# Decay attention and gated convolution on one core: products in 64-column tiles, a shorter decay chain, small first units and a fixed order

## The chip, the core and the metric

The kernel runs on one core of a Trainium2 chip. The metric is device time in microseconds (us) of one launch. The core has a matrix engine (TensorE, PE in the profile, with its weight loads as PEld), a vector engine (VectorE, DVE), an activation engine (ScalarE, ACT), GpSimd (POOL) and a queue that issues all transfers of this kernel (SyncE, SP). All data are float32; the weights come in as float64 and are turned into float32 on the core.

## What is computed

The reference, cut to what matters. It has B, H, S, D = 4, 8, 768, 48; the model width is H*D = 384.

```python
mag = np.sqrt(a_re * a_re + a_im * a_im)
scale = np.minimum(mag, 0.999) / (mag + 1e-06)
a_re_n, a_im_n = (a_re * scale, a_im * scale)
for t in range(S):                     # S_re, S_im: [B, H, D, D], from zero
    new_re = ar * S_re - ai * S_im
    new_im = ar * S_im + ai * S_re
    kv = np.einsum('bhd,bhe->bhde', k[:, :, t], v[:, :, t])
    S_re, S_im = (new_re + kv, new_im)
    y[:, :, t] = np.einsum('bhd,bhde->bhe', q[:, :, t], S_re)
# x = y with the heads side by side: [B, S, 384]
gate_pre += conv_w[k][None, None, :] * xp[:, k:k + S, :]      # five taps, causal
gate = 1.0 / (1.0 + np.exp(-gate_pre))
val = x @ w_val
out = gate * val @ w_out
```

The complex decay a is turned into sums of logarithms and angles over time. With these, keys are divided and queries multiplied by the running decay (96 numbers each for a head: a cosine and a sine part), and the recurrence becomes attention in chunks of 128 steps with a state of 96 by 48 that is carried from chunk to chunk.

## The kernel before, in words

**Units.** The 32 pairs of batch and head are worked in units: seven of four heads, then two of two heads. A unit goes through a chain of steps, each a stream that is named by a letter. A and X load squares, take logarithms and exponentials of a_re and a_im (lines 271 to 302). R makes the angle with an arctangent, adds up over time (`add_up`, line 241), adds the sums of the partitions ahead by a product with a triangular matrix (`offset`, line 247), and turns the angle into turns (lines 304 to 362). S takes sine and cosine, E the exponentials of the summed logarithm (lines 364 to 379), B multiplies keys (`kx`) and queries (`qx`, in the tile `trig`) with them (lines 381 to 420). ScalarE does the functions, VectorE the rest. The scaled keys also go to DRAM (`kd`) and come back as `kn` with time on the partitions. T transposes `kx` and `qx` on TensorE (`transpose`, line 436), and ScalarE copies the results out of PSUM into `kq` (line 437).

**Chunks.** Of each unit's six chunks of 128 steps, `s` makes the scores (`scores`, line 456; one product of 128 by 128 for each head), `k` masks them (`masked`, VectorE), `t` adds the chunk's keys and values to the state (`state`, line 488; 96 stationary columns, 48 streamed), and `y` makes the output (`output`, line 468: two products of 48 stationary columns for each head; heads with an even number write PSUM partitions 0 to 47, the others 64 to 111). Scores have one PSUM bank (PSC = 1).

**The second layer.** C is the convolution on VectorE (five passes over 128 by 768 for each of three column blocks of a batch), G the sigmoid, M the two products of 384 by 384 (`project`, lines 539 and 571: `pv` with w_val and `po` with w_out, three stationary blocks of 128 by 128, each streaming 384), W the conversion of the weights.

**Order.** `ORDER` is a string of these letters. It tells in which order the steps are written into the program. The framework's scheduler may then move instructions of an engine against each other, as long as the data allow it. `in_turn` fixes the order of some ScalarE instructions only, to keep the function tables together. Transfers are written where their buffers come free (`loads`, `vloads`).

Each float32 product is run as two passes on TensorE, so one written product gives two MATMUL records in the profile; a transpose gives one. TensorE works on the array either as a whole or as column tiles: 48 stationary columns at PSUM partition 0 and 48 at partition 64 lie in two tiles of 64 columns.

If an input lies outside the range for which the sums hold, a flag (`guard`, from the sums in `over`) leads to a slow step-by-step version at the end (`step_by_step`); the given inputs don't set it.

Of the kernel before, what the change touches and what calls it, by code (L numbers as in the profile page):

```python
# [10 lines left out]
F32 = mybir.dt.float32  # L11
# [11 lines left out]
    "WWAWWWAWWWWAXXXXRRRRRRRRRWRRWRRWRRWRWRRWRSSEEBWBWWWWBWWWBTTTTWWWWWWWWWWsksyWksWAAAXXXWtXWyWksRWt"  # L23
    "WRyWksWRWtRWyWksRWtWRWykRWWtRWyCCRCCRtCRCARRARSSEEBBBAXXXXRRRRRRRRRRRRRRBTTTTtsksykskysktysSSEEB"
    "ktBBBysktyTtyTTtTACsksAkstCyAXXXXRRRRRRRRRRRRRCRSSEEBkstCAyCAkstCCCyAXXBCXCkstXyCCGMMMMMMMMMMMMM"
    "ktyBtyRRRRRRMRRRMBTTTTtstksyksytRkRMRRMsRSSyMtMkMMsyMtMkMMsCyEMtkCyAAAXXXEBBBBCXRRRRRRRRRRRRRRCT"
    "TCTSTttskskysytkytsksAytSEACCCCCCCCCCCksCAXyCGMMMMMMMMtEBMMBMMMXkyXXBRRRMRRMRRMRMRBTTTTstksykyst"
    "RMRRMRksMRSSEEyMtMAMksMyMtACCBMCCCCksAXytXkBytXBXRRRRRRRRRBTTTTsttkskysksyksRAAtAXXXXRyksRtRCCCy"
    "kCCRSSECCCCCCCGCCCCCCMMMMMMMMMMMMMtRREBBBRRRyRBTRRRRtRTtsksRMRMRMMMMMMMyCCCCCtkCMsMyktMMsyktsykt"
    "SSEEBBBBTsyktyTskstyyksytksytksytksytkytCCCCCCCCCCCCGCCCCCCGCCCCCCGMMMMMMMMMMMMMMMMMMMMMMMMMM"  # L30
)
TURN = 2.0 ** 24
# [3 lines left out]
SS_MIN = 0.25  # L36
RHO_MAX = 1.5
RE_MIN = 0.75
SS_MAX = 1.8
# [3 lines left out]
def kernel(  # L43
# [12 lines left out]
    nc = tc.nc  # L56
# [18 lines left out]
    LB, MAINB, TMPB, KB, PSC, SMB, SSB, ZB, XB, KNB, VB, YB = 6, 3, 1, 6, 1, 2, 3, 4, 2, 3, 3, 2  # L75
    BOTH = 1
    W1, W2 = 4, 6
# [16 lines left out]
    last = [None]  # L94

    def in_turn(ins):

        if last[0] is not None:
            tc.add_manual_dep(
                ins.ins, last[0].name,  # L100
                mybir.DependencyInfo(mybir.DependencyClass.NoSync, mybir.DependencyReason.DATA),
                reason="one table set after the other",
            )
        last[0] = ins.ins
        return ins

    loaded = [None]

    def table_set(name):
        if loaded[0] != name:  # L110
            in_turn(nc.scalar.preload_act_table_set(name))  # L111
            loaded[0] = name
# [3 lines left out]
    def load(u, nm):  # L116
        b, h0, g = units[u]
        tl = tiles.setdefault(u, {"v": []})
        if nm == "v":
            for hn in range(2):  # L120
                vt = ld.tile([C, HN, g, D], F32, name="v_in", bufs=VB)
                for h in range(g):
                    nc.sync.dma_start(
                        out=vt[:, :, h, :],
                        in_=v[b, h0 + h, hn * HS:(hn + 1) * HS].rearrange("(n i) e -> i n e", i=C),
                    )
                tl["v"].append(vt)
        else:
            t = ld.tile([P, 2, g, JH, D], F32, name=f"{nm}_in", tag="in")
            for f in range(2):  # L130
                nc.sync.dma_start(  # L131
                    out=t[:, f].rearrange("p h j d -> p h (j d)"),
                    in_={"ar": a_re, "ai": a_im, "k": k, "q": q}[nm][b, h0:h0 + g, f * HS:(f + 1) * HS].rearrange(
                        "h (p j) d -> p h (j d)", j=JH
                    ),
                )
            tl[nm] = t
# [9 lines left out]
    load(0, "ai")  # L147

# [3 lines left out]
    for f in range(2):  # L152
# [7 lines left out]
    mask = const.tile([C, C], F32, name="mask")  # L160
    nc.gpsimd.memset(mask, 1.0)
    nc.gpsimd.affine_select(
        out=mask, in_=mask, pattern=[[1, C]], compare_op=ALU.is_ge, fill=0.0,
        base=0, channel_multiplier=-1,
    )
    b_tiny = const.tile([P, 1], F32, name="b_tiny")
    nc.gpsimd.memset(b_tiny, 2.0 ** -60)
    b_re = const.tile([P, 1], F32, name="b_re")
    nc.gpsimd.memset(b_re, RE_MIN)
    b_ss = const.tile([P, 1], F32, name="b_ss")  # L170
    nc.gpsimd.memset(b_ss, -math.log(SS_MAX))
    over = const.tile([P, 4, NU], F32, name="over")
    flag = const.tile([1, 1], I32, name="flag")
    junk = const.tile([P, G * D * J], BF16, name="junk")
# [4 lines left out]
    b_rho = const.tile([P, 1], F32, name="b_rho")  # L179
    nc.gpsimd.memset(b_rho, math.log(2.0 ** 31 / RHO_MAX))  # L180

# [54 lines left out]
    for t in y_ps:  # L236
        nc.vector.memset(t, 0.0)
# [8 lines left out]

    def offset(x, mat, gd):

        off = ps_m.tile([P, 512], F32, name="off", tag="mm")
        for f in range(2):  # L250
            nc.tensor.matmul(off[:, f * gd:(f + 1) * gd], mat[:, f], x[:, JH - 1, f], start=True, stop=True)  # L251
        return off[:, :2 * gd]

    tmps = []
# [9 lines left out]
    def new_tmp(ne):  # L264
        tmps.append(False)
        return work.tile([P, 2, ne], F32, name="tmp", bufs=TMPB), len(tmps) - 1

    def tmp_free():
        return len(tmps) < TMPB or tmps[-TMPB]

    def prep_a(u):

        b, h0, g = units[u]
        tl = tiles[u]
        tl["main"] = work.tile([P, 2, JH, 2, g * D], F32, name="main", bufs=MAINB)
        main, mf, mj = views(u)
        nc.scalar.activation(mj[:, 1], jm(tl["ar"]), AF.Square)
        yield
        nc.scalar.activation(mj[:, 0], jm(tl["ai"]), AF.Square)
        yield  # L280
        nc.vector.scalar_tensor_tensor(
            out=mf[:, 0], in0=mf[:, 1], scalar=SS_MIN, in1=mf[:, 0], op0=ALU.max, op1=ALU.add
        )

    def prep_x(u):

        b, h0, g = units[u]
        tl = tiles[u]
        main, mf, mj = views(u)
        while not tmp_free():  # L290
            yield "wait"
        tmp, mine = new_tmp(g * D * J)
# [3 lines left out]
        in_turn(nc.scalar.activation(tmp[:, 1], mf[:, 1], AF.Exp, bias=b_rho, scale=-0.5))  # L296
        yield
        in_turn(nc.scalar.activation(tmp[:, 0], mf[:, 0], AF.Exp, bias=b_inv, scale=-0.5))
        yield
        rho = tmp[:, 1].rearrange("p (j x d) -> p j x d", j=JH, x=2 * g)  # L300
        nc.vector.tensor_tensor(out=mj[:, 1].bitcast(I32), in0=rho, in1=jm(tl["ai"]), op=ALU.mult)
        tl["tmp"] = tmp, mine

    def prep_r(u):
# [3 lines left out]
        gd, ne = g * D, g * D * J  # L308
# [3 lines left out]
        in_turn(nc.scalar.activation(mf[:, 1], mf[:, 1].bitcast(I32), AF.Arctan, scale=RHO_MAX / 2.0 ** 31))  # L312
        yield
        tmp, mine = tl["tmp"]
        nc.scalar.activation(junk[:, :ne], mf[:, 0], AF.Relu, bias=b_ss, accum_out=over[:, 1, u:u + 1])  # L315
        nc.vector.scalar_tensor_tensor(
            out=mf[:, 0], in0=mf[:, 0], scalar=2.0 * math.log(0.999), in1=tmp[:, 0],
            op0=ALU.min, op1=ALU.subtract,
        )
        tmps[mine] = True  # L320
        nc.scalar.activation(
            junk[:, :ne], tl["ar"].rearrange("p f h j d -> p (f h j d)"), AF.Relu, bias=b_re, scale=-1.0,
            accum_out=over[:, 0, u:u + 1],
        )
        done["ai", u] = True
        yield
        if u >= BOTH:
            yield from add_up(main)
        else:
            yield from add_up(main[:, 1])  # L330
# [7 lines left out]
        yield  # L338
        if u < BOTH:
            yield from add_up(main[:, 0])  # L340
        off = offset(main[:, 0], dmat, gd)
# [11 lines left out]
        )  # L353
        yield
# [9 lines left out]
    def prep_s(u):  # L364
        main, mf, mj = views(u)
        trig = tiles[u]["trig"]
        table_set("trig_and_small")
        in_turn(nc.scalar.activation(
            trig[:, :, 0, :], mf[:, 1].bitcast(I32).rearrange("p (x d) -> p x d", d=D), AF.Sin, scale=RADIAN
        ))  # L370
        yield
        in_turn(nc.scalar.activation(trig[:, :, 1, :], trig[:, :, 1, :], AF.Sin, bias=b_quart))

    def prep_e(u):
        main, mf, mj = views(u)
        table_set("natural_log_exp_and_others")
        in_turn(nc.scalar.activation(mf[:, 1], mf[:, 0], AF.Exp, scale=-0.5, accum_out=over[:, 2, u:u + 1]))
        yield
        in_turn(nc.scalar.activation(mf[:, 0], mf[:, 0], AF.Exp, scale=0.5, accum_out=over[:, 3, u:u + 1]))

    def prep_b(u):
# [20 lines left out]
        kd = dram.tile([S, g, C2], F32, name="kd")  # L402
# [5 lines left out]
        while not all(2 * u + i < KNB or kn_read(2 * u + i - KNB) for i in range(2)):  # L408
            yield "wait"
        tl["kn"] = []  # L410
        for hn in range(2):
            kn = qkp.tile([C, HN, g, C2], F32, name="kn", bufs=KNB)
            nc.sync.dma_start(
                out=kn.rearrange("i n h c -> i n (h c)"),
# [540 lines left out]
```

## Time and profile before

| | |
|---|---|
| median of 3 runs | 353.44 us (352.72 to 356.88) |
| the profiled execution | 352.57 us, its span 350.9 us |
| PE busy | 291.3 us, 83% of the span |
| PEld busy | 221.7 us, 63% |
| ACT busy | 266.7 us, 76% |
| DVE busy | 254.8 us, 73% |
| moved by DMA | 54.73 MB, mean 156 GB/s |

Times are read from the start of the span. A group's row gives line, engine, operation, the tiles, out and in, the count, then busy us and mean ns of one, and then the idle time of the engine ahead of them with what ended it. A row of the chain of waits gives the start, how long the chain stays with these instructions, and which they are. "(+1 forms)" means that the group holds instructions of a second size, here those of the two-head units.

### The profile page before, as it was taken

How to read it: one execution, taken by the hardware profiler on the slowest of the kernel's cores; microseconds unless marked ns; L12 is line 12 of the kernel's file. 1: busy time of each engine (PE TensorE's matmuls, PEld its weight loads, DVE VectorE, ACT ScalarE, POOL GpSimd, SP SyncE). 2: the span in 40 equal slices, each digit the busy share in tenths (PEclk: the TensorE clock that was granted, in tenths of full speed). 3: DMA queues.
4: the chain of work that ended last, by engine and by line, in shares of the span. 5: the costliest groups of instructions: out<-in, count | busy, mean ns of one | idle time of the engine just before them, and what ended most of it. 6: DMA issues, size and time to landing. Idle time of an engine off the chain costs nothing.

```text
span 350.9 us, 5801 instructions
## 1 busy us (share of the span) xinstructions
PE 291.3 (83%) x2154; PEld 221.7 (63%) x2154; DVE 254.8 (73%) x322; ACT 266.7 (76%) x454; POOL 2.5 (1%) x23
## 2 busy tenths in 40 slices
PE   0030298958988998999999999999999999999992
PEld 0020187748767775777887767777877775676551
DVE  0599987899685998788989786788479736356610
ACT  3958989998998989599879986998996375362201
POOL 2000000000000000000000000000000000000000
PEclk9999999989999999999999999999999999999998
DMA  7993781269579549745674576458410532520102
GB/s 230 370 243 67 241 239 61 61 196 356 124 214 256 148 117 296 220 110 174 194 210 102 151 218 212 95 186 275 92 39 2 153 102 92 164 48 21 62 32 67
DMA packets 84562, 54.73 MB, mean 156 GB/s; under 512 B 31024, under 2 KB 83760, under 8 KB 84528
## 3 DMA queue, kind: packets, MB, share of 16 engines
q1 hardware_dynamic: 84528, 54.30, 53.2%
q8 instruction: 19, 0.31, 0.4%
q14 instruction: 15, 0.12, 0.1%
HBM read 35.40 MB, written 14.16 MB: 141 GB/s over the span
## 4 chain that ended last, share of the span: by engine, by line
PE 67%; ACT 14%; DVE 6%; DMA 5%; SPq 3%; issue 2%; ACTq 0%
PE pv L539 13%; PE po L571 12%; PE pt L436 11%; PE sc L459 10%; PE S_ps L495 7%; PE y_ps L477 5%; PE y_ps L480 5%; PE off L251 3%; SPq L131 2%; DMA q_in<-in_q_dram 2%; ACT main L294 2%; ACT L111 2%; DMA kn<-kd 1%; ACT kq L437 1%; ACT junk L315 1%
## 5 line engine op out<-in xcount | busy, mean ns | idle before, releaser
L437 ACT COPY kq<-pt 96x384 f32<-96x384 f32 x128 | 55.8, 478 | 6.6 <-PE pt L436 6.1
L459 PE MATMUL sc<-kq 96*128 96x128 f32 x384 | 58.3, 282 | 2.0 <-DVE sm L464 2.0
L459 PEld LDWEIGHTS sc<-kq 96*128 96x128 f32 x384 | 50.6, 193 | 10.5 <-DVE sm L464 4.8
L539 PE MATMUL pv<-xT,wv_sb 128*128 128x384 f32 x144 | 54.8, 498 | 0.0
L571 PE MATMUL po<-wo_sb,z 128*128 128x384 f32 x144 | 51.7, 496 | 1.0 <-DVE z L545 1.0
L464 DVE TENSOR_TENSOR sm<-sc,mask 128x512 f32<-128x512 f32 (+1 forms) x54 | 34.0, 629 | 25.5 <-PE sc L459 15.7
L524 DVE SCALAR_TENSOR_TENSOR z<-xT,cw_sb,z 128x768 f32<-128x768 f32 (+1 forms) x60 | 50.6, 854 | 1.1
L436 PE MATMUL pt<-ident,kx 128*96 128x128 f32 x192 | 34.0, 288 | 15.1 <-DVE kx L394 12.2
L477 PE MATMUL y_ps<-kq,S_sb 96*48 96x128 f32 x320 | 39.8, 286 | 3.9 <-ACT y_sb L481 3.0
L480 PE MATMUL y_ps<-sm,v_in 128*48 128x128 f32 x384 | 42.1, 275 | 0.1
L436 PE MATMUL pt<-ident,trig 128*96 128x128 f32 x192 | 34.0, 286 | 6.4 <-DVE trig L394 5.0
L495 PE MATMUL S_ps<-v_in,kn 128*96 128x48 f32 x320 | 36.8, 247 | 1.3 <-DMA kn<-kd 0.8
L495 PEld LDWEIGHTS S_ps<-v_in,kn 128*96 128x96 f32 x320 | 34.0, 167 | 6.0 <-issue 4.5
L571 PEld LDWEIGHTS po<-wo_sb,z 128*128 128x128 f32 x144 | 25.7, 190 | 17.1 <-DVE z L545 2.3
L436 PEld LDWEIGHTS pt<-ident,kx 128*96 128x96 f32 x192 | 21.5, 132 | 21.7 <-DVE kx L394 12.9
L111 ACT ACT_TABLE_LOAD x25 | 32.1, 1283 | 1.2 <-PEq L939 0.8
L481 ACT COPY y_sb<-y_ps 112x256 f32<-112x256 f32 (+1 forms) x54 | 18.6, 345 | 18.2 <-PE y_ps L480 17.8
L436 PEld LDWEIGHTS pt<-ident,trig 128*96 128x96 f32 x192 | 21.7, 132 | 16.1 <-issue 6.9
L539 PEld LDWEIGHTS pv<-xT,wv_sb 128*128 128x128 f32 x144 | 24.4, 190 | 9.9 <-issue 0.9
L576 ACT COPY ot<-po 128x384 f32<-128x384 f32 x24 | 11.4, 478 | 24.1 <-PE po L571 23.8
L477 PEld LDWEIGHTS y_ps<-kq,S_sb 96*48 96x48 f32 x320 | 21.1, 122 | 13.6 <-ACT y_sb L481 5.6
L480 PEld LDWEIGHTS y_ps<-sm,v_in 128*48 128x48 f32 x384 | 27.4, 123 | 3.1 <-issue 0.7
(81 smaller groups left out, 394.5 us busy)
## 6 DMA issues: line engine op xcount, KB each, us to landing
kd<-kx SPq DMA_DIRECT2D x14, 576.0 KB, 3.5
kn<-kd SPq DMA_DIRECT2D x14, 576.0 KB, 4.7
v_in<-in_v_dram SPq DMA_DIRECT2D x64, 72.0 KB, 2.7
out_dram<-ot SPq DMA_DIRECT2D x24, 192.0 KB, 2.3
ar_in<-in_a_re_dram SPq DMA_DIRECT2D x14, 288.0 KB, 4.0
ai_in<-in_a_im_dram SPq DMA_DIRECT2D x14, 288.0 KB, 4.8
k_in<-in_k_dram SPq DMA_DIRECT2D x14, 288.0 KB, 3.4
q_in<-in_q_dram SPq DMA_DIRECT2D x14, 288.0 KB, 4.6
```

What stands on the lines that cost most here:

```text
L111: in_turn(nc.scalar.preload_act_table_set(name))
L436: nc.tensor.transpose(pt[:C2, j, :], src[:, j, f, h, :], ident)
L437: nc.scalar.copy(tj[:, s, f], pt[:C2].rearrange("c j p -> c p j"))
L459: nc.tensor.matmul(sc[:, h, :], self.part(0, h, n), self.part(1, h, n), start=True, stop=True)
L464: nc.vector.tensor_tensor(out=sm, in0=sc[:, :g], in1=mask[:, None, :].to_broadcast([C, g, C]), op=ALU.mult)
L477: nc.tensor.matmul(o, self.S_sb[n - 1][:, h * D:(h + 1) * D], self.part(1, h, n), start=True, stop=False)
L480: nc.tensor.matmul(o, vt[:, h, :], sm[:, h, :], start=(n == 0), stop=True)
L481: nc.scalar.copy(self.y_sb[:112, :, (n % HN) * C:(n % HN + 1) * C], yp[:112, :g // 2 * C].rearrange("e (r t) -> e r t", t=C),)
L495: nc.tensor.matmul(self.S_ps[:C2, h * D:(h + 1) * D], kn[:, h, :], vt[:, h, :], start=(n == 0 and h == 0), stop=(n == NCH - 2), skip_group ...
L524: nc.vector.scalar_tensor_tensor(out=z, in0=xT[:, c, EXT + t0 - t:EXT + t0 - t + n], scalar=cw_sb[:, TAPS - 1 - t, c:c + 1], in1=z, op0=AL ...
L539: nc.tensor.matmul(pv[:, :n], wv_sb[:, ci, c * P:(c + 1) * P], xT[:, ci, EXT + t0:EXT + t0 + n], start=(ci == 0), stop=(ci == NT - 1),)
L571: nc.tensor.matmul(po[:, :DM], z[ci][:, m:m + P], wo_sb[:, ci, :], start=(ci == 0), stop=(ci == NT - 1))
```

## The change

**Column tiles.** `in_two` writes a product of 128 stationary columns as two of 64, one to PSUM partitions 0 to 63 and one to 64 to 127. It is used for `pv`, `po` and `off`. A state product of 96 columns becomes one of 64 and one of 33 (one zero column is added behind `kn`). Only the transposes keep the whole array.

**Scores.** For each head, keys are cut in two halves of 64. The first half is multiplied with all 128 queries, the second with the last 64 queries only; the quarter left out is masked anyway. For half of the heads the two halves of the keys change places on the partitions, so that both tiles get equal work. `v` and `kn` are loaded with the same exchange, in two transfers where there was one, and the mask has two kinds. The PSUM tile of the scores is cleared once at the start.

**The decay chain.** Before: squares of a_re and a_im, their sum, one logarithm over both parts, two exponentials, and two passes (into `junk`) that watch the range. After: ln(a_re), its negative exponential, the ratio a_im / a_re, its square (which also gives the sum that watches the range), ln(1 + square), an exponential, and two combining steps on VectorE.

**Units.** There are ten: two of two heads, six of four, two of two. `X`, `R` and `A` have a second stream each (`x`, `r`, `a`) for units with an odd number, and `tmp` has two buffers.

**Order.** `ORDER` is new; a T step is now a quarter of a head; L, V, N, D and O place the loads, the loads of v, the loads of `kn`, the copies of y into `xT` and the output transfers. At the end a loop chains all instructions of PE, ACT, DVE and SP in the order in which they were written, so the scheduler moves nothing on these.

TensorE in the middle of the run, before: the work of a few chunks (`sc` scores, `y_ps` output, `S_ps` state) with part of a projection (`po`). "x4" counts written products.

```order
L571 MATMUL po<-wo_sb,z 128x384
L459 MATMUL sc<-kq 128x128 x4
L477 MATMUL y_ps_131<-kq,S_sb 48x128
L480 MATMUL y_ps_131<-sm,v_in 48x128
L477 MATMUL y_ps_131<-kq,S_sb 48x128
L480 MATMUL y_ps_131<-sm,v_in 48x128
L477 MATMUL y_ps_131<-kq,S_sb 48x128
L480 MATMUL y_ps_131<-sm,v_in 48x128
L477 MATMUL y_ps_131<-kq,S_sb 48x128
L480 MATMUL y_ps_131<-sm,v_in 48x128
L495 MATMUL S_ps<-v_in,kn 96x48
L459 MATMUL sc<-kq 128x128 x4
```

And a place early in the program after, where a two-head unit's chunk is worked: scores (lines 444 and 445), a state step (lines 484 and 485), two groups of three transposes, and the start of an output step.

```order
L444 MATMUL sc_ps_134<-kq 64x128
L445 MATMUL sc_ps_134<-kq 64x64
L444 MATMUL sc_ps_134<-kq 64x128
L445 MATMUL sc_ps_134<-kq 64x64
L484 MATMUL S_ps<-v_in,kn 64x48
L485 MATMUL S_ps<-v_in,kn 33x48
L484 MATMUL S_ps<-v_in,kn 64x48
L485 MATMUL S_ps<-v_in,kn 33x48
L416 MATMUL pt<-ident,kx 96x128 x3
L416 MATMUL pt<-ident,trig 96x128 x3
L464 MATMUL y_ps_133<-kq,S_sb 48x128
L467 MATMUL y_ps_133<-sm,v_in 48x128
```

A score and a state product have each become two (those of the projections too); of the work on the whole array only the transposes are left, and they stand between products in column tiles.

ScalarE at the start of the program, before: the first unit's functions, up to its first exponential of the summed logarithm (line 377).

```order
L111 ACT_TABLE_LOAD
L277 ACTIVATE main<-ar_in 128x1152
L279 ACTIVATE main<-ai_in 128x1152
L277 ACTIVATE main<-ar_in 128x1152
L294 ACTIVATE main<-main,b_tiny 128x2304
L279 ACTIVATE main<-ai_in 128x1152
L296 ACTIVATE tmp<-main,b_rho 128x1152
L298 ACTIVATE tmp<-main,b_inv 128x1152
L111 ACT_TABLE_LOAD
L315 ACTIVATE junk,over<-main,b_ss 128x1152
L312 ACTIVATE main<-main 128x1152
L213 ACTIVATE cvt<-raw 128x384
```

And after (line 263 is ln(a_re), 267 the exponential, 274 the square, 277 the second logarithm, 297 the arctangent):

```order
L99 ACT_TABLE_LOAD
L263 ACTIVATE main<-ar_in 128x576
L267 ACTIVATE tmp<-main 128x576
L274 ACTIVATE tmp,over<-main 128x576
L277 ACTIVATE tmp<-tmp,b_one 128x576
L263 ACTIVATE main<-ar_in 128x576
L267 ACTIVATE tmp<-main 128x576
L282 ACTIVATE tmp<-main,b_inv 128x576
L99 ACT_TABLE_LOAD
L297 ACTIVATE main<-main 128x576
L274 ACTIVATE tmp,over<-main 128x576
L99 ACT_TABLE_LOAD
```

The instructions are half as wide, two units are worked side by side from the start, and there are more table loads.

The diff, cut to its core:

```diff
-    units = [(b, h0, G) for b in range(B) for h0 in range(0, H, G)][:-1] + [(B - 1, H - G, 2), (B - 1, H - 2, 2)]
+    units = [(0, 0, 2), (0, 2, 2)] + [(b, h0, G) for b in range(B) for h0 in range(0, H, G)][1:-1]
+    units += [(B - 1, H - G, 2), (B - 1, H - 2, 2)]
...
+    def rows(h, g):
+        return ((0, 0, C),) if h < g // 2 else ((0, C // 2, C // 2), (C // 2, 0, C // 2))
...
+    def in_two(out, lhsT, rhs, **kw):
+        for c in (0, 64):
+            nc.tensor.matmul(out[c:c + 64], lhsT[:, c:c + 64], rhs, **kw)
...
-        in_turn(nc.scalar.activation(mf, mf, AF.Ln, bias=b_tiny))
-        in_turn(nc.scalar.activation(tmp[:, 1], mf[:, 1], AF.Exp, bias=b_rho, scale=-0.5))
-        in_turn(nc.scalar.activation(tmp[:, 0], mf[:, 0], AF.Exp, bias=b_inv, scale=-0.5))
+        nc.scalar.activation(mj[:, 0], jm(tl["ar"]), AF.Ln)
+        nc.scalar.activation(tmp, mf[:, 0], AF.Exp, scale=-1.0)
+        nc.vector.tensor_tensor(
+            out=mj[:, 1], in0=tmp.rearrange("p (j x d) -> p j x d", j=JH, x=2 * g), in1=jm(tl["ai"]), op=ALU.mult
+        )
+        nc.scalar.activation(tmp, mf[:, 1], AF.Square, accum_out=over[:, 0, u:u + 1])
+        nc.scalar.activation(tmp, tmp, AF.Ln, bias=b_one)
+        nc.vector.scalar_tensor_tensor(out=mf[:, 0], in0=mf[:, 0], scalar=2.0, in1=tmp, op0=ALU.mult, op1=ALU.add)
+        nc.scalar.activation(tmp, mf[:, 0], AF.Exp, bias=b_inv, scale=-0.5)
...
-            for h in range(self.g):
-                nc.tensor.matmul(sc[:, h, :], self.part(0, h, n), self.part(1, h, n), start=True, stop=True)
+            for h in [x for i in range(m) for x in (i, i + m)]:
+                k, q = self.part(0, h, n), self.part(1, h, n)
+                lo, hi = (0, half) if h < m else (half, 0)
+                nc.tensor.matmul(sc[lo:lo + half, h, :], k[:, :half], q, start=True, stop=True)
+                nc.tensor.matmul(sc[hi:hi + half, h, half:], k[:, half:], q[:, half:], start=True, stop=True)
...
+                nc.tensor.matmul(self.S_ps[:64, cols], kn[:, c0:c0 + 64], vt[:, h, :], **at_h)
+                nc.tensor.matmul(self.S_ps[64:C2 + 1, cols], kn[:, c0 + 64:c0 + C2 + 1], vt[:, h, :], **at_h)
...
+    for ins in nc.cur_bb.bb.instructions:
+        if ins.engine not in IN_ORDER:
+            continue
+        if ins.engine in before:
+            tc.add_manual_dep(
+                ins, before[ins.engine].name,
+                mybir.DependencyInfo(mybir.DependencyClass.NoSync, mybir.DependencyReason.DATA),
+                reason="the order that the steps are written in",
+            )
+        before[ins.engine] = ins
```

More of the change, by code (lines that the diff above doesn't have):

```diff
@@ L92 @@
     dram = fast.enter_context(tc.tile_pool(name="dram", bufs=2, space=DRAM))
[L94 to L105, printed above, removed]
     loaded = [None]
@@ L159 @@
     nc.vector.tensor_scalar_mul(dturn, dmat, TURN / (2.0 * PI))
-    mask = const.tile([C, C], F32, name="mask")
+    mask = const.tile([C, 2, C], F32, name="mask")
     nc.gpsimd.memset(mask, 1.0)
[L162 to L172, printed above, removed]
+    for kind, r0, i0 in ((0, 0, 0), (0, C // 2, C // 2), (1, 0, C // 2), (1, C // 2, 0)):
+        nc.gpsimd.affine_select(
+            out=mask[r0:r0 + C // 2, kind], in_=mask[r0:r0 + C // 2, kind], pattern=[[1, C]],
+            compare_op=ALU.is_ge, fill=0.0, base=-i0, channel_multiplier=-1,
+        )
+    b_one = const.tile([P, 1], F32, name="b_one")
+    nc.gpsimd.memset(b_one, 1.0)
+    over = const.tile([P, 3, NU], F32, name="over")
     flag = const.tile([1, 1], I32, name="flag")
-    junk = const.tile([P, G * D * J], BF16, name="junk")
     b_quart = const.tile([P, 1], F32, name="b_quart")
@@ L235 @@
     y_ps = [ps_y.tile([P, 512], F32, name=f"y_ps{i}") for i in range(1)]
-    for t in y_ps:
+    sc_ps = [ps_s.tile([C, 4, C], F32, name=f"sc_ps{i}") for i in range(PSC)]
+    for t in y_ps + sc_ps:
         nc.vector.memset(t, 0.0)
@@ L262, in views @@
         return main, main.rearrange("p s j f x -> p s (j f x)"), main.rearrange("p s j f (h d) -> p s j (f h) d", h=g)
[L264 to L283, printed above, removed]
     def prep_x(u):
@@ L311, in prep_r @@
             table_set("trig_and_small")
-        in_turn(nc.scalar.activation(mf[:, 1], mf[:, 1].bitcast(I32), AF.Arctan, scale=RHO_MAX / 2.0 ** 31))
+        nc.scalar.activation(mf[:, 1], mf[:, 1], AF.Arctan)
         yield
[L314 to L330, printed above, removed]
+        yield from add_up(main)
+        done["sums", u] = True
         off = offset(main[:, 1], dturn, gd)
@@ L353, in prep_r, with prep_a @@
         )
+    def prep_a(u):
+        b, h0, g = units[u]
+        gd = g * D
+        main, mf, mj = views(u)
+        off = offset(main[:, 0], dmat, gd)
         yield
@@ L407, in prep_b @@
             )
-        while not all(2 * u + i < KNB or kn_read(2 * u + i - KNB) for i in range(2)):
-            yield "wait"
         tl["kn"] = []
[L411 to L414, printed above, removed]
-                in_=kd[hn * HS:(hn + 1) * HS].rearrange("(n i) h c -> i n (h c)", i=C),
-            )
-            tl["kn"].append(kn)
+        done["kd", u] = True
         yield
@@ L695, in has_x @@
     def has_x(b, c, t):
-        n = -(-t // HS) * HN - 1
+        n = -(-t // HS) - 1
         return all(
-            done.get(("y", u, n)) for u in range(NU) if units[u][0] == b and units[u][1] * D < (c + 1) * P
+            done.get(("D", u, n)) for u in range(NU) if units[u][0] == b and units[u][1] * D < (c + 1) * P
         )
@@ L803, in advance @@
-            r = chunk(key)
-        else:
-            r = next(gens[key], "end") is None
-        loads()
-        vloads()
-        return r
+            return chunk(key)
+        if key in "LVNDO":
+            return move(key)
+        return next(gens[key], "end") is None
     def finished():
-        return done.get(("M", len(pieces) - 1))
-    loads()
-    vloads()
+        return done.get(("M", len(pieces) - 1)) and at["O"] == len(outs)
     for key in ORDER:
```

317 lines of the change are left out of this document (182 added, 135 removed).

## The prediction

> **What bounds the kernel now.** I read the page first, with its 40 slices (8.8 us each):
>
> ```profile
> span 350.9 us, 5801 instructions
> PE   0030298958988998999999999999999999999992
> DVE  0599987899685998788989786788479736356610
> ACT  3958989998998989599879986998996375362201
> PE 67%; ACT 14%; DVE 6%; DMA 5%; SPq 3%; issue 2%; ACTq 0%
> ```
>
> TensorE has almost nothing for four slices, gaps up to slice 15, and is full from slice 16 (140 us) on; the last row, the chain that ended last, is two thirds TensorE. So there are two stages: the units' preparation (ACT, DVE) sets the pace first, TensorE afterwards. The busy times by stretch say which engine leads in the first (start and end, length, busy us and count of each engine, clock, DMA):
>
> ```profile
> 20.00:60.00 40.00, 19.55 (x126) 16.75 (x127) 37.22 (x58) 33.89 (x53) 0.22 (x2) 1.00 0.60 166
> 60.00:100.00 40.00, 34.05 (x332) 29.32 (x330) 33.21 (x32) 37.60 (x60) 0.00 (x0) 0.96 0.60 173
> 140.00:180.00 40.00, 39.44 (x313) 31.07 (x312) 32.78 (x32) 32.53 (x59) 0.11 (x1) 1.00 0.62 182
> ```
>
> From 60 to 100 us ScalarE works 94% and VectorE 83%; from 140 on TensorE works 99%. The chain in order of time, in the second stage, gives the price of each kind of product:
>
> ```profile
> 164.63 0.89 PE sc L459 x8
> 165.52 0.36 PE y_ps L477 x4
> 165.88 0.22 PE y_ps L480 x4
> 166.10 0.25 PE y_ps L477 x4
> 166.35 0.22 PE y_ps L480 x4
> ...
> 169.36 0.30 PE S_ps L495 x2
> ...
> 175.57 0.79 PE pt L436 x6
> 176.37 0.64 PE S_ps L495 x8
> ...
> 218.13 0.66 PE pt L436 x6
> ...
> 338.54 5.82 PE po L571 x18
> ```
>
> Per record: scores 0.89/8 = 0.111 us (128 columns streamed), transposes 0.66/6 = 0.110, `po` 5.82/18 = 0.323 (384 columns), state 0.64/8 = 0.080. Output products also stream 128 columns but take 0.22/4 = 0.055: heads alternate between two column tiles, and the two run side by side, each at the price of a score. State streams only 48 columns, so its 0.080 is the load of 96 stationary columns. Where the array goes from whole to tiles the first four take 0.36 for 0.25, and back, two state records take 0.30 for 0.16: 0.11 and 0.14 us, 0.125 per switch.
>
> **Part by part.** *Scores.* Two heads give each tile one product of 128 and one of 64 streamed columns, in two passes: 2 × (0.110 + 0.055) = 0.33 us for two heads, 0.165 each, against 4 × 0.111/2 = 0.222. Bounds: this, if they pair as the output products do, and 0.222 if not, which is 8 us more in the sum below. I take 0.165.
>
> *State.* 64 and 33 stationary columns load in two tiles. By columns, the longer takes 0.080 × 64/96 = 0.053; with a little on top 0.055 for a pass, against 0.080. Nothing in the trace shows 32 records for four heads come that fast: the densest rows above are the outputs, 0.055 per record. At that spacing a pass of two records takes 0.11, which is 11 us more below. I take 0.055, nearest to the rows of the outputs, where two tiles load and stream at once. The Trainium skill has a rule against so many small records (TensorE: Matmul & The Clock Gate, section "Wait — 56ns, not 53.3ns?"): without hardware decode the sequencer's own code spends about 62 ns on each matmul. By that a pass of two takes 0.124, and state would be 14 us more in the sum, an estimate from that page. The 0.055 per output record speaks against it, though only over 0.9 us at a time.
>
> *`pv`, `po`, `off`.* Twice the records, half as wide, two at once: 0.161 per record, the sum unchanged. They gain nothing by themselves. Their cover is that the tiles overlap.
>
> *Switches.* In the order after, 73 switches lie behind the first transpose of the fifth unit (unit 4); the order before has 78. Only transposes switch now, but they come in small groups, so this part is about nil.
>
> *ScalarE.* Rows of what goes and stays, for eight full units' worth (seven full, two half):
>
> ```profile
> L111 ACT ACT_TABLE_LOAD x25 | 32.1, 1283 | 1.2 <-PEq L939 0.8
> L277 ACT ACTIVATE main<-ar_in 128x1152 f32<-128x1152 f32 (+1 forms) x9 | 9.5, 1057 | 3.4 <-DMA ar_in<-in_a_re_dram 3.4
> L315 ACT ACTIVATE junk<-main,b_ss 128x1152 bf16<-128x1152 f32 (+1 forms) x9 | 10.3, 1144 | 0.0
> L321 ACT ACTIVATE junk<-ar_in,b_re 128x1152 bf16<-128x1152 f32 (+1 forms) x9 | 10.4, 1150 | 0.0
> ```
>
> One square (9.5) and both range passes (10.3, 10.4) go, 30 us with nothing in return; 34 table loads instead of 28 give back 6 × 1.28 = 8. Some 22 us less, 2.8 for each unit, in the very engine that led the first stage.
>
> *VectorE.* The chain keeps its number of full passes (two combining steps stay two), so a unit costs what it did:
>
> ```profile
> L394 DVE TENSOR_TENSOR kx<-trig,main 128x2304 f32<-128x2304 f32 (+1 forms) x9 | 20.5, 2282 | 0.6 <-PE pt L436 0.6
> L244 DVE TENSOR_TENSOR main<-main 128x768 f32<-128x768 f32 (+1 forms) x20 | 15.7, 794 | 4.0 <-ACT main L312 3.6
> L301 DVE TENSOR_TENSOR main<-tmp,ai_in 128x1152 int32<-128x1152 f32 (+1 forms) x9 | 11.0, 1217 | 0.4 <-ACT tmp L296 0.4
> L347 DVE TENSOR_SCALAR main<-main 128x1152 uint32<-128x1152 uint32 (+1 forms) x9 | 6.2, 684 | 0.0
> L356 DVE TENSOR_SCALAR off<-off 128x384 f32<-128x384 f32 (+1 forms) x9 | 4.6, 515 | 0.8 <-PE off L251 0.8
> L464 DVE TENSOR_TENSOR sm<-sc,mask 128x512 f32<-128x512 f32 (+1 forms) x54 | 34.0, 629 | 25.5 <-PE sc L459 15.7
> L524 DVE SCALAR_TENSOR_TENSOR z<-xT,cw_sb,z 128x768 f32<-128x768 f32 (+1 forms) x60 | 50.6, 854 | 1.1
> L198 DVE SCALAR_TENSOR_TENSOR cvt<-raw,cvt 128x384 uint32<-128x384 uint32 x6 | 3.2, 549 | 0.0
> ```
>
> Per full unit: (2 × 20.5 + 15.7 + 7 × 11.0 + 6.2 + 4.6)/8 = 18.1 us, seven being the steps like line 301. With ScalarE relieved, this engine sets the first stage.
>
> *The head.* Before, the first transpose starts at 38 us:
>
> ```profile
> 4.91 1.16 ACT L277 ACTIVATE main<-ar_in 128x1152 f32<-128x1152 f32 x1 [2.81 <-DMA ar_in<-in_a_re_dram]
> 37.99 0.87 PE L436 MATMUL pt<-ident,kx 128*96 128x128 f32 x3 [11.92 <-DVE kx L394]
> ```
>
> After, ScalarE has up to the exponential that `kx` of unit 0 needs: five table loads (6.4), 16 functions of half width, at half of 1.06 to 1.15 and a little on top 0.65 each (10.4), two short ones of the weights (1.0, an estimate), from about 4.9 on, that is to 22.7; the two VectorE steps of half width (0.7 and 1.3) give 24.7. Waits between the engines inside this can add 3.
>
> *DMA and the pinned queues.* v and `kn` cost SP 84 more issues, and each state step waits for the last of three `kn` transfers instead of one. SP's own waits show what stands in line behind such a queue:
>
> ```profile
> SPq L577 <- ACT ot L576: 26.0, 12, 7.3
> ```
>
> An output transfer that waits for ScalarE holds up what is issued behind it, a `kn` among it, now in a place that nothing moves. Its cover is the work TensorE has ahead of the state. I cost it at nothing; if the cover is gone I count a us for each of ten units, an estimate between nothing and the row's longest wait, 7.3.
>
> **The sum.** The chain goes over VectorE up to `kx` of unit 4, then over TensorE. Between `kx` of unit 0 and of unit 4, VectorE has in the order after: three and a half units' worth of preparation (63), three column blocks of the convolution (12 passes of 0.93, three first ones of 0.53: 13), 20 masks (8 of 0.6 and 12 of 0.35: 9), three and a half of six weight pieces (9), gating (2): 96 us. ScalarE has 86 there counted in the same way, so VectorE leads. At 95% (its 93% from 20 to 60 us, and ScalarE's 94% when that led, are the rows) it takes 101: transposes of unit 4 start at 126 us. Bounds: 100% gives 120, the 83% of the second row gives 140.
>
> From there TensorE has 132 head-chunks of scores (21.8), 104 of state at two passes (11.4), 488 output records (26.8), 240 transposes (26.4), 492 of `pv` and `po` (79.2), `off` (3.9), 73 switches (9.1): 178.6 us. The same prices for what is behind 175.57 us before (unit 4's first transpose) give 159, while the chain takes 344.4 − 175.6 = 168.8: 10 us are waits. A pinned order may keep between all and none of these; I take half, 5. With the 350.9 − 344.4 = 6.5 us of the end: 126 + 178.6 + 5 + 6.5 = 316 us of span, and 1.7 around it (352.57 − 350.9): 318 us. The median before lies 0.9 above its profiled execution, which I leave out.
>
> **Rivals.** *Records can't be fed fast enough.* Behind unit 4's first transpose the scores, outputs and state are 1432 records, in 60 us by my prices, 0.042 each. The output block of 16 took 1.05 with its switch, 0.066 each, and nothing denser stands in the trace. At 0.066 they take 95, 35 more; the wide `pv` and `po` records between them let a queue fill, so half is likelier: 335 us, at worst 353. For it: twice the records. Against: within a block 0.055 was held.
> By the page named at the state (62 ns) it would be 29 us before any buffering, an estimate.
>
> *The pinned order stalls.* Each engine now waits in line for its next written step. If VectorE works 75% in the first stage, kx of unit 4 comes at 153 us, and all of the 10 us and 5 more come back: 353, no change. Against: the stage before had 83% with VectorE second.
>
> *The tiles take turns* (slower; the change doesn't do what it says). If two halves of one `pv` product, which stream the same columns, don't overlap, 492 records cost 0.323: 79 us more, 397 in all. It decides from half of that on (42 us more passes 360). For it: only output products, each with columns of its own, show the overlap. Against: those overlap fully, with up to four records of the same tile written ahead of the other tile's.
>
> *The order fits better than I think*: VectorE without gaps and no waits behind, below 307; below 302 only if prices fall too.
>
> **Chances.** My forecast, 302 to 340: 0.67; below 302: 0.08; feeding: 0.12; stalls: 0.08; turns: 0.05. The range takes in the forecast's own bounds (120 + 178.6 + 0 + 8.2 = 307 and 140 + 178.6 + 10 + 8.2 = 337) and feeding up to 344: 302 to 344. A measurement tells 2% from no change, 346 or 360 us. Faster: 0.67 + 0.08 + 0.10 of feeding + 0.02 of stalls = 0.87; within 2%: 0.02 + 0.06 = 0.08; slower: 0.05.
>
> **What would show it.** Right: eight score records and their eight short ones in about 0.66 us; 16 state records in 0.44; 36 `po` records in 5.8; first transpose near 25 us; TensorE full from about 126 us; VectorE busier than ScalarE from 25 to 125 us. Wrong: score or state blocks at 0.055 per record or more (feeding); 36 `po` records in 11 us (turns); VectorE under 80% up to unit 4 (stalls); a state step that waits for `kn` for more than a us (the SP queue).

## The result and the profile after

The changed kernel takes 394.55 us (median of 4 runs, 392.33 to 399.87), the kernel before beside it 353.6 us. The ratio is 1.112 (95% interval 1.101 to 1.123): 11% slower, where 318 us were forecast. A few executions of these kernels, one of the four here among them, took over 1.5% longer at a lower granted clock than the others; all times and differences from here on are medians without them, 393.18 us for the changed kernel. The profiled execution took 393.18 us. Its page, as for before: busy time, the slices (9.8 us each here), the granted clock, and the chain that ended last.

```profile
span 391.0 us, 8175 instructions
PE 290.2 (74%) x3234; PEld 206.0 (53%) x3234; DVE 259.3 (66%) x339; ACT 253.0 (65%) x458; POOL 5.4 (1%) x43
PE   0125583872984999899198999867988988968994
DVE  3699999786382999478357986229579544736440
ACT  6789999894564496995269978751777573334111
PEclk9999988796668799999679999986999999996999
PE 33%; ACT 17%; DMA 16%; DVE 15%; SPq 13%; issue 4%; DVEq 0%; ACTq 0%
```

No engine sets the time. Around 90 to 100, 120 and 190 us all three drop together (TensorE to 2, 4 and 1 tenths, VectorE, at the first place a slice later, to 3, 2 and 3, ScalarE to 4, 4 and 2), so something stops all of them. TensorE's share of the chain has fallen from 67% to 33%; transfers have 16% (5% before) and SP's queue 13% (3% before). The stretches that the prediction used:

```profile
20.00:60.00 40.00, 21.45 (x195) 15.75 (x196) 38.47 (x60) 37.84 (x64) 0.30 (x3) 0.96 0.62 168
60.00:100.00 40.00, 22.92 (x251) 16.77 (x251) 29.97 (x36) 30.58 (x55) 0.30 (x3) 0.79 0.62 160
100.00:140.00 40.00, 31.89 (x374) 26.23 (x372) 26.30 (x27) 22.82 (x41) 0.20 (x2) 0.78 0.52 143
140.00:180.00 40.00, 37.19 (x410) 24.91 (x406) 30.42 (x34) 35.15 (x54) 0.30 (x3) 1.00 0.55 149
```

From 20 to 60 us VectorE works 96%, as forecast; then 75% and 66%, and ScalarE with it (76% and 57%). What SP's queue waits for (line of the waiting transfer, what it waits for, us in total, times, longest) says where the stop is:

```profile
SPq L397 <- DMA kn<-kd: 56.7, 20, 4.9
SPq L797 <- ACT ot L563: 31.6, 11, 7.3
SPq L499 <- ACT y_sb L468: 15.1, 5, 8.6
SPq L377 <- DVE kx L367: 12.4, 3, 7.8
```

The first row did not exist before. Line 397 is the transfer of `kn`, and what it waits for is a transfer of `kn`. `load_kn` fills one tile in three pieces for two groups of heads: the first group on all 128 partitions, the second on partitions 64 to 127 and 0 to 63, in the columns behind the first group's. No byte is written twice, but in the program the second group's first transfer waits until the first group's has landed, 20 times, 2.8 us each. The kernel before, with one transfer of `kn` a half unit, has no wait of this kind. SP's own time line from 77 to 102 us (start, length, what it issued), and the chain of waits in the same place:

```profile
77.21 14.05 SPq L397 DMA_DIRECT2D kn<-kd  x9
91.35 1.84 SPq L499 DMA_DIRECT2D xT<-y_sb  x3
93.23 3.85 SPq L126 DMA_DIRECT2D v_in<-in_v_dram  x6
97.13 1.15 SPq L109 DMA_DIRECT2D ar_in<-in_a_re_dram  x2
98.38 1.25 SPq L377 DMA_DIRECT2D kd<-kx  x2
99.67 2.56 SPq L109 DMA_DIRECT2D ai_in<-in_a_im_dram  x2
```

```profile
86.80 3.21 DMA kn<-kd
90.03 0.57 SPq L397
...
99.67 1.18 SPq L109
...
100.90 7.10 DMA ai_in<-in_a_im_dram
...
108.12 1.37 DVE main L269
```

Nine `kn` transfers hold the queue for 14 us. Behind them stand the loads of v and those of a_re and a_im for a unit that has not begun; a_im is issued at 99.67, lands at 108.00, and only then does VectorE begin that unit. So the wait is not paid by TensorE's state step, which uses `kn`, but here by the next unit's first step. Over the whole run the copies of y into `xT`, for which the convolution waits, pay more: VectorE's largest wait, in the changed kernel and in the version A of the experiments, in which `kn` has no such wait and SP fewer transfers:

```profile
DVE z L508 <- DMA xT<-y_sb: 38.6, 9, 9.5
```

```profile
DVE z L502 <- DMA xT<-y_sb: 10.2, 4, 4.3
```

TensorE runs dry behind the stop, and from 60 to 140 us its granted clock is 0.78 to 0.79, where before had 0.96 from 60 to 100.

### The profile page after: what moved, and what is told of

The parts are those of the page before. It is cut to its first block, busy times and chain, and to the rows that moved or that the text cites. A ratio compares the mean times of both kernels' runs of the same rounds, so it can differ in the third digit from the quotient of the medians.

```text
span 391.0 us, 8175 instructions
## 1 busy us (share of the span) xinstructions
PE 290.2 (74%) x3234; PEld 206.0 (53%) x3234; DVE 259.3 (66%) x339; ACT 253.0 (65%) x458; POOL 5.4 (1%) x43
## 4 chain that ended last, share of the span: by engine, by line
PE 33%; ACT 17%; DMA 16%; DVE 15%; SPq 13%; issue 4%; DVEq 0%; ACTq 0%
PE po L237 8%; DMA kn<-kd 6%; PE pv L237 5%; PE pt L416 5%; SPq L126 4%; PE sc_ps L444 4%; DVE z L511 4%; PE y_ps L467 3%; SPq L109 3%; PE y_ps L464 3%; ACT L99 3%; SPq L499 3%; DMA ai_in<-in_a_im_dram 3%; DMA xT<-y_sb 3%; ACT kq L417 3%
## 5 line engine op out<-in xcount | busy, mean ns | idle before, releaser
L451 DVE TENSOR_TENSOR sm<-sc_ps,mask 128x512 f32<-128x512 f32 (+1 forms) x60 | 34.7, 579 | 35.4 <-PE sc_ps L445 35.2
L237 PE MATMUL po<-wo_sb,z 128*64 128x384 f32 x288 | 52.3, 501 | 7.6 <-DVE z L532 7.6
L444 PE MATMUL sc_ps<-kq 96*64 96x128 f32 x384 | 48.6, 299 | 12.5 <-DVE sm L451 12.3
L237 PE MATMUL pv<-xT,wv_sb 128*64 128x384 f32 x288 | 49.2, 487 | 0.0
L444 PEld LDWEIGHTS sc_ps<-kq 96*64 96x64 f32 x384 | 35.5, 150 | 22.9 <-DVE sm L451 16.9
L445 PE MATMUL sc_ps<-kq 96*64 96x64 f32 x384 | 47.2, 238 | 0.0
L484 PE MATMUL S_ps<-v_in,kn 128*64 128x48 f32 x320 | 33.8, 242 | 14.8 <-DMA v_in<-in_v_dram 12.5
L445 PEld LDWEIGHTS sc_ps<-kq 96*64 96x64 f32 x384 | 42.2, 149 | 0.0
L484 PEld LDWEIGHTS S_ps<-v_in,kn 128*64 128x64 f32 x320 | 28.6, 156 | 20.9 <-issue 10.4
L237 PEld LDWEIGHTS po<-wo_sb,z 128*64 128x64 f32 x288 | 22.0, 140 | 28.6 <-DVE z L532 13.1
L237 PEld LDWEIGHTS pv<-xT,wv_sb 128*64 128x64 f32 x288 | 21.3, 137 | 20.9 <-issue 18.2
```

The source lines that it names most:

```text
L237: nc.tensor.matmul(out[c:c + 64], lhsT[:, c:c + 64], rhs, **kw)
L444: nc.tensor.matmul(sc[lo:lo + half, h, :], k[:, :half], q, start=True, stop=True)
L445: nc.tensor.matmul(sc[hi:hi + half, h, half:], k[:, half:], q[:, half:], start=True, stop=True)
L451: nc.vector.tensor_tensor(out=two(sm), in0=two(sc[:, :g]), in1=mask[:, :, None, :].to_broadcast([C, 2, g // 2, C]), op=ALU.mult)
L484: nc.tensor.matmul(self.S_ps[:64, cols], kn[:, c0:c0 + 64], vt[:, h, :], **at_h)
```

## Experiments

All edits are against the changed kernel unless the diff's heading says otherwise. "A" below is the version of e4. The kernel before was run beside each group: 351.83 us beside e1 to e4, 350.80 (one execution) beside e5 to e8, 351.97 beside e9 to e11 and e4 again, 351.45 beside e12 to e15.

**e1: two tiles for `kn`.** Each group of heads gets its own tile; the same 60 transfers, none waits for another.

```diff
+        for h in (0, m):
+            flat = qkp.tile([C, HN * m * C2 + 1], F32, name=f"kn{h > 0:d}", bufs=KNB)
...
+                nc.sync.dma_start(out=kn[i0:i0 + n], in_=src[i1:i1 + n, :, h * C2:(h + m) * C2])
```

> kn of a half lies in two tiles, one for each pair of head groups, so the second transfer no longer waits for the first to land; nothing else differs. Queue theory (the SP queue stands still 57 us in 20 waits of a kn transfer for another kn transfer, and what is behind it comes late): most of the 57 us goes, 340 to 365 us. Pinned-order theory (the order of the steps itself doesn't fit the real durations on PE, ACT and DVE): under 2% gained, 386 us or more.

Measured: 360.69 us, ratio to before 1.024 (1.008 to 1.041), 32 us less than the changed kernel. SP's waits begin with these rows; the wait of `kn` for `kn` is gone, and these two are about 5 us longer than before the edit:

```profile
SPq L797 <- ACT ot L563: 36.8, 9, 8.3
SPq L499 <- ACT y_sb L468: 19.8, 7, 8.0
```

The wait accounts for 32 of the 40 us by which the changed kernel is slower, but not for the gain that is missing.

**e2: SP's queue not pinned.**

```diff
-IN_ORDER = (mybir.EngineType.PE, mybir.EngineType.Activation, mybir.EngineType.DVE, mybir.EngineType.SP)
+IN_ORDER = (mybir.EngineType.PE, mybir.EngineType.Activation, mybir.EngineType.DVE)
```

> Only the SP queue's instructions are left out of the pinned order; PE, ACT and DVE keep theirs. Queue theory: the kn waits stay (about 57 us), the scheduler may put other transfers ahead of them, so some part comes back, 375 to 395 us. If it is the place of the transfers in the queue and not the waits: 350 us or less. Pinned-order theory on PE, ACT and DVE: no change.

Measured: 359.96 us (one execution), between the two expectations. The wait is still in the program, but the scheduler puts other transfers ahead of the waiting one, so that it costs 12.5 us in 13 instead of 56.7 in 20:

```profile
SPq L797 <- ACT ot L563: 40.9, 12, 12.1
...
SPq L397 <- DMA kn<-kd: 12.5, 13, 2.2
```

So the cost needs both together, a wait for a landing and an order in which nothing goes past it.

**e3: nothing pinned** (`IN_ORDER = ()`).

> No engine is pinned; the scheduler places all steps as in the kernel before. Pinned-order theory: 320 to 345 us, since the column tiles and the shorter decay chain are still there. Queue theory: the waits of kn for kn are still there, 375 us or more.

Measured: 379.73 us, ratio 1.078 (1.055 to 1.102). The first transpose comes at 33.7 us and ScalarE has 37% of the chain. With SP free, pinning TensorE, ScalarE and VectorE is worth 20 us here (359.96 against 379.73); pinning SP as well costs 33.

**e4, or A: no exchange of halves.** `kn` and v come in one transfer each, as before; the first half of the keys is always in the lower tile, so a head's short score product always falls to the upper one, and the mask follows. Everything else stays. SP issues 295 transfers instead of 367 (283 before).

```diff
-        return ((0, 0, C),) if h < g // 2 else ((0, C // 2, C // 2), (C // 2, 0, C // 2))
+        return ((0, 0, C),)
...
-                lo, hi = (0, half) if h < m else (half, 0)
+                lo, hi = 0, half
```

> The two halves of the keys no longer change places for half of the heads: v and kn are loaded in whole transfers again (one kn transfer per half unit, four of v), no kn waits for a kn, and some 72 issues go (0.63 us each, 45 us of the queue). Scores cost TensorE up to 11 us more, since one tile has all the long products. Queue theory: 335 to 360 us. Pinned-order theory: 390 us or more.

Measured: 345.82 us, ratio 0.982 (0.968 to 0.996); again, beside e9 to e11:

> e4 (no exchange of key halves: whole transfers of v and kn, everything else as changed) once more, to settle whether it beats the kernel before: 344 to 348 us, ratio 0.97 to 0.99.

346.62 us, ratio 0.985 (0.979 to 0.991). It is the fastest version, faster than both kernels, though than the kernel before by less than 2%: 47 us less than the changed kernel, 15 less than e1. Its slices and chain:

```profile
PE   0114658488689989899998999999999999989993
PE 36%; ACT 20%; DVE 19%; DMA 11%; SPq 6%; issue 5%; ACTq 0%; DVEq 0%
```

**e10 and e11: the two halves of the exchange's price, each added to A.** e10 puts back the wait: `kn` in two column halves of one tile, 20 transfers more. e11 puts back 72 transfers, of `kn` and v, but no wait: the pieces are cut by partitions (the diff shows those of `kn`).

```diff
+        for x in (slice(0, g // 2 * C2), slice(g // 2 * C2, g * C2)):            # e10
+            nc.sync.dma_start(out=kn[:, :, x], in_=src[:, :, x])
...
+        for i0, i1 in ((0, 64), (64, 96), (96, C)):                              # e11
+            nc.sync.dma_start(out=kn[i0:i1], in_=src[i0:i1])
```

> e4 with kn of each half loaded in two transfers that share partitions, so the second waits for the first to land, as in the changed kernel: 20 issues and 20 waits of about 2.8 us more on the SP queue, nothing else. Queue theory: 370 to 385 us. If the exchange cost its time otherwise (smaller packets, number of issues): 350 us or less.

> e4 with as many transfers as the changed kernel (v and kn cut by partitions, 72 issues more) but no wait between them and no exchange. If the SP queue is a bound by its issues too: 72 x 0.62 = 45 us of issuing, of which a third to a half shows, 358 to 370 us. If only the waits count: 345 to 349 us.

Measured: e10 367.00 us (one execution), 20 over A and 3 below the range of its queue theory; e11 360.13 us (ratio 1.024, 1.014 to 1.035), 13.5 over A, as expected. In e10 the wait shows again, now the first row:

```profile
SPq L395 <- DMA kn<-kd: 57.8, 20, 4.4
```

By e11's rate, 13.5/72 = 0.19 us for each transfer, e10's 20 further transfers are about 4 of its 20 us, so the wait alone is worth some 16 there, and 32 in the changed kernel, where the queue holds 72 transfers more than in A. The wait (16 to 32) and the transfers (13.5) together are 30 to 46 of the 47 us between A and the changed kernel; as they add on top of each other, no finer split is shown. e1 and e11 have the same 367 transfers, none of which waits for another of its tile, and take the same time (360.69 and 360.13 us), though only e1 has the balanced scores, and with them `kn` in half rows; what these two are worth, one against the other, is not separated.

**e5, e6, e8: another queue.** e5 is the changed kernel with the `kn` transfers issued by GpSimd, their wait kept; e6 is A with the output transfers issued by GpSimd; e8 is e1 with both there. The edit is `nc.sync.dma_start` to `nc.gpsimd.dma_start` at these places.

> The changed kernel with one edit: the kn transfers are issued from GpSimd's queue. The second transfer still waits for the first to land, but only kn stands behind it. Queue theory (what hurts is everything that stands behind the waiting transfer on the SP queue): 335 to 362 us. Late-kn theory (what hurts is that the state gets its kn two landings late, wherever it is issued): 385 us or more.

> e4 (no exchange of key halves) with the 24 output transfers issued from GpSimd's queue. In e4 the SP queue still stood 43 us before output transfers that wait for ScalarE. If these hold up loads that are needed: 330 to 341 us. If the places in the pinned order cover them: 343 to 348 us, as e4.

> e1 (kn in two tiles, equal work for both column tiles kept) with kn and the output transfers issued from GpSimd's queue, 84 issues fewer on SP. Queue theory: SP has about as many issues as the kernel before and no wait for kn or outputs, so the forecast's sum should nearly hold, 318 to 338 us. If something else than the queue holds the kernel back: 345 us or more.

Measured: e5 358.53 us, 35 less than the changed kernel, though `kn` still waits for `kn`, on a queue where nothing else stands behind it:

```profile
POOL kn L397 <- DMA kn<-kd: 45.1, 19, 6.7
```

So a late `kn` costs little here (e5 is 2 us below e1, where `kn` doesn't wait for `kn`); what stands behind it in SP's queue does. e6, 348.48 us, is A within a per cent (and half a us over its second case). A's largest wait in SP's queue, that of the output transfers for ScalarE, is thus covered:

```profile
SPq L791 <- ACT ot L557: 43.5, 10, 10.1
```

e8, 363.46 us, came in its second case: without a wait of `kn` for `kn`, without the outputs and with 84 issues fewer, something else than SP's queue holds it, and it is no better than e1 or e5. On GpSimd's queue, ahead of `kn`, the outputs now wait for ScalarE:

```profile
POOL out_dram L797 <- ACT ot L563: 74.8, 15, 14.8
```

That this is why e8 gains nothing is argued, not shown.

**e9 and e7: what the tiles are worth.** e9 is A with scores (the masked quarter among them), state and projections on the whole array; the pinned order stays. e7 is the kernel before with the products in tiles, without exchange, and its own order.

```diff
-        for c in (0, 64):                                                        # e9
-            nc.tensor.matmul(out[c:c + 64], lhsT[:, c:c + 64], rhs, **kw)
+        nc.tensor.matmul(out, lhsT, rhs, **kw)
```

> e4 with every product on the whole array again (scores with the masked quarter, state of 96 columns), order, units and decay chain as changed. By the prices of the prediction the column tiles save 8 us of state and about 14 us of switches around output products, little else: 355 to 370 us. If the tiles are worth nothing in this order: 343 to 349 us.

> The kernel before, with its scheduler, units, decay chain and loads, and only the products changed: off, pv, po, scores (masked quarter left out, no exchange of halves) and state in 64-column tiles. By my prices the state saves 8 us on TensorE, scores and projections nothing: 342 to 349 us against 352. If twice the records cost TensorE something in feeding them: 355 us or more.

Measured: e9 358.12 us (ratio 1.019, 1.011 to 1.026), so the tiles are worth 11.5 us in A. e7: 359.02 us beside 350.80, 8 us slower where 3 to 10 us of gain were expected. The time lies in the expectation's case for feeding, but that isn't the cause: its blocks of 16 state records take 0.39 us from the first start to the last (median of five), A's 0.44. Its scheduler mixes transposes with other products, so that TensorE changes between the whole array and tiles 162 times, where before has 130 and A 118 (counted in the traces). At the prediction's 0.125 us the 32 more than before are 4 us; the rest of e7's miss is not explained.

**e12 to e15: what holds A back.** The question was whether SP's queue also holds the 20 to 30 us that A lacks against the sum. e12 lets ScalarE issue A's 80 copies of y into `xT`, e13 lets GpSimd issue A's loads of v, e15 does both, e14 is e1 with the copies issued by ScalarE.

```diff
-                    nc.sync.dma_start(
+                    nc.scalar.dma_start(                                         # e12, e14, e15
```

> e4 with the 80 copies of y into xT issued from ScalarE's queue, 50 us of issuing off the SP queue. If the SP queue still holds e4 back: 330 to 341 us. If ScalarE pays as much for issuing as the queue gains: 346 to 360 us. If the queue is no bound any more and issuing is cheap on ScalarE: 344 to 348 us.

> e4 with the 64 loads of v issued from GpSimd's queue, about 40 us of issuing off the SP queue. If the SP queue still holds e4 back: 332 to 342 us. If not: 344 to 350 us.

> e1 (exchange kept, kn in two tiles, 367 issues) with the 80 copies into xT issued from ScalarE's queue. If the number of issues on the SP queue is what sets e1 (361) apart from e4 (346): 340 to 350 us. If it is the smaller packets or the number of transfers on any queue: 356 us or more.

> Both edits of e12 and e13: 144 of e4's issues leave the SP queue. If the queue was what kept e4 20 us over the forecast's sum with undivided scores (326 us): 325 to 335 us. If the first stage (VectorE up to the fifth unit) and waits on TensorE do: 342 us or more.

Measured: e12 388.91 us (ratio 1.111, 1.106 to 1.116), e14 387.83, e15 388.87; e13 351.39 (0.999, 0.994 to 1.003). The first three are far slower than A; e12 lies above all its cases, and e14 and e15 lie in open ranges, for a reason that none names: an issue occupies ScalarE itself. The group of e12's copies by the queue of ScalarE (shortest, median and longest, in ns):

```profile
L493 ACTq DMA_DIRECT2D xT<-y_sb x80: 511/601/1172, 71.1 to 364.8; - x80
```

80 × 0.60 = 48 us of an engine that the first stage needs, and behind it TensorE's transposes, which wait 26.0 us for its copies out of PSUM (8.3 in A); e12 is 42 us over A. These runs therefore say nothing on SP's queue. e13 says something: 64 transfers fewer on SP, and 5 us slower than A, a little over the upper end of its second case. Nothing here shows that the number of transfers on SP holds A back; what issuing from GpSimd costs by itself is not separated.

## Why the prediction was wrong, step by step

The points of the prediction's sum, as times in the spans of four executions. The first three rows come from the first transposes, the fifth unit's first transposes and TensorE's last record:

| us | forecast | after | e1 | A |
|---|---|---|---|---|
| first transpose | 24.7 | 28.2 | 27.8 | 27.6 |
| transposes of unit 4 start | 126 | 157.6 | 143.4 | 138.8 |
| TensorE's last record starts | 309.6 | 384.7 | 351.1 | 337.3 |
| span | 316 | 391.0 | 357.5 | 343.8 |

The rows for unit 4, of the changed kernel and of A (times of the first and last start):

```profile
L416 PE MATMUL pt<-ident,kx x3: 272/273/315, 157.6 to 157.9; 128*96 128x128 f32 x3
```

```profile
L410 PE MATMUL pt<-ident,kx x3: 273/273/315, 138.8 to 139.0; 128*96 128x128 f32 x3
```

**The step that failed** is *DMA and the pinned queues*: "I cost it at nothing; if the cover is gone I count a us for each of ten units". The exchange, net of the balance that it gives the scores, measured 47 us: the wait of `kn` for `kn` 32 (e1; 16 when added alone, e10), and the further transfers 13.5 (e11). The step looked at the wrong waiter. It asked whether the state step would wait for the last of three `kn` transfers, and that it hardly does, twice in the run, though the longer time is over the prediction's sign of a us:

```profile
PE S_ps L485 <- DMA kn<-kd: 2.1, 2, 1.4
```

It named the queue behind a waiting output transfer, but not that `kn` transfers could wait for each other, nor that next units' loads stand behind them. Nor did it give 84 transfers a price in SP's time. At 0.61 us each (the median of the loads of v, in ns between shortest and longest) they are some 51 us in all, an estimate; of the issuing of 72 of them e11 shows 13.5 to reach the end:

```profile
L126 SPq DMA_DIRECT2D v_in<-in_v_dram x96: 413/610/1807, 7.5 to 350.9; - x96
```

The sign to look for was in the code of `load_kn`: several transfers into one tile, in a queue whose order is fixed. The Trainium skill (Perfetto Trace Analysis, section "DMA Instruction — HWDGE (DVE, Sync)") puts the semaphore wait of a transfer into the sequencer, ahead of the making of its descriptors, and says that the DMA engines themselves do not wait; this trace agrees, with 14.05 us in which the queue issued nothing but nine `kn` transfers.

**The head** came at 28.2 us, 3.5 over the forecast and 0.5 beyond its allowance for waits; before had 38.

**The first stage.** VectorE leads up to 60 us as forecast. From `kx` of unit 0 to the end of `kx` of unit 4, by the same columns as above, in the changed kernel and in A:

```profile
28.10:152.20 124.10, 86.19 (x915) 64.06 (x917) 98.92 (x123) 93.35 (x160) 0.90 (x9) 0.85 0.57 153
```

```profile
27.60:133.20 105.60, 81.75 (x912) 62.44 (x914) 98.54 (x122) 92.71 (x160) 1.27 (x9) 0.92 0.67 179
```

In the changed kernel VectorE is busy 98.9 us of 124.1, 80% and not 95%, at the edge of the sign that the prediction gave for stalls, and `kx` of unit 4 ends at 152.2 us, the *pinned order stalls* rival's 153 for 75%. That rival had the nearest mechanism; its price, 353 (by its sum a span, so 355 as a time), was too low because it let only 15 us come back behind unit 4, where the queue went on holding up v, `xT` and a later unit's loads: TensorE took 227.1 us from there to its last record, against 178.6 + 5 forecast.

In A, without the queue's trouble, VectorE is busy 98.5 us of 105.6, 93%: the forecast's 96 us at 95%, 101, nearly held. A is nevertheless 13 us late at unit 4. Its first transpose comes 3 us late, VectorE's stretch is 4 to 5 us longer, and unit 4's transposes start 5.6 us behind its `kx`, where the sum had them start at once: TensorE is working all that time (5.60 us of 5.60), on output, state and projection products that stand ahead of them in the written order.

```profile
133.20:138.80 5.60, 5.60 (x66) 3.77 (x62) 5.08 (x4) 3.85 (x6) 0.00 (x0) 1.00 0.78 243
```

Behind it, A took 198.5 us, where the sum with undivided scores (132 × 0.057 = 7.5 more) gives 191. These 20 us are A's distance from the forecast (318 + 7.5, against 346). The split is read from the trace; no run tests it. Of the last 7 us, the cause stays open: the granted clock is 1.00 there, and e6 and e13 give no sign that the output waits or the number of transfers in SP's queue are behind them.

**TensorE's prices held**, so *feeding* and *tiles take turns* are refuted. From the end of the changed kernel's chain:

```profile
360.14 1.94 PE pv L237 x12
362.07 0.06 PE sc_ps L444
362.13 0.06 PE sc_ps L445
362.19 0.11 PE sc_ps L444 x2
362.30 0.03 PE sc_ps L445
362.33 0.06 PE sc_ps L444
...
379.36 5.82 PE po L237 x36
```

36 `po` records take 5.82 us, the forecast's 5.8, and 12 `pv` 1.94, 0.161 each: two tiles side by side, not in turns (11 us). The eight score records of a two-head unit, of which the chain names six, take 0.33 us by their starts (361.89 to 362.23), 0.042 each, the forecast's 0.33; blocks of 16 that nothing holds up take 0.67 to 0.72 to the next record in tiles, where the forecast had 0.66. A state step of four heads is 16 records, as the sum has it (the prediction's part on state says 32). Those that nothing holds up take 0.45 us to the start of an output product and 0.54 to 0.60 to that of a transpose, which has a switch in it: the forecast's 0.44 and its 0.125 for a switch, not feeding's 0.88. The Trainium skill's 62 ns for each matmul (TensorE: Matmul & The Clock Gate, section "Wait — 56ns, not 53.3ns?") is not seen: the score records come every 42 to 45 ns and the state records, where no switch follows, every 28. Its section "Back-to-back issue gap" has about 25 ns as the floor of an issue otherwise; the state blocks come near that.

**Switches** were about nil, as said: 118 in all, before 130.

**ScalarE** became less busy by 14 us (253.0 for 266.7), where the prediction counted some 22, and **VectorE** busier by 4.5 (259.3 for 254.8), where it counted nothing. Both are small beside the 47 us of the exchange.

So TensorE's parts were priced rightly, and a resource that had no term in the sum decided. With the exchange left out, the direction is right (A's intervals, 0.968 to 0.996 and 0.979 to 0.991, lie below 1), but only 5 to 6 us of the gain are there (351.97 − 346.62 and 351.83 − 345.82), where the sum gives 35, or 28 without the balance of the scores.

## What to carry to other kernels

Before a change splits transfers, count them and what each waits for, on the queue that issues them: several transfers into one tile can be made to wait for each other although they share no byte, and in a queue with a fixed order everything behind pays, here the next unit's loads rather than the user of the tile. Give the issuing queue a term of its own in the sum (issues × about 0.6 us here, and each wait for a landing), as for any engine. A separate tile for each piece took 32 us of the loss away, whole transfers of `kn` and v 47.

## What was not expected of the hardware

An issue costs the engine that makes it: 0.60 us on ScalarE's queue (80 of them made the kernel 42 us slower), 0.61 on SP's (the loads of v), 0.76 on GpSimd's (v in e13: 64 issues, 48.8 us, mean 764 ns).

```profile
L126 POOL DMA_DIRECT2D v_in<-in_v_dram x64 | 48.8, 764 | 149.0 <-PE y_ps L461 137.8 <-PE pt L410 6.6 <-PE S_ps L479 4.6
```

The Trainium skill (Trainium Kernel Development and Optimization, section "Key Constraints") says that issuing from several engines only saves the sequencer's issue time; in e12 the 48 us that SP saved were spent by ScalarE, which computes, and the kernel became 42 us slower.

Two 64-column tiles reach 0.042 us for a float32 score record (128 and 64 columns streamed by turns) and 0.028 for a state record (48 streamed), in the changed kernel's trace, with as many weight loads as products. In the changed kernel the granted clock falls to 0.78 where TensorE has gaps (57% busy from 60 to 100 us), and at 100 to 140 us it is as low with 80% busy; the runs don't separate cause and effect there.
